# Inverse softmax sums by way of DRAM, K loaded for four heads, q and K turned in pairs

## The chip, the cores and the metric

The kernel runs on one core of one Trainium2 chip. The core has five engines that run side by side: TensorE (PE in the profile, with its weight loads as PEld), VectorE (DVE), ScalarE (ACT), GpSimd (POOL) and SyncE (SP), which issues the DMAs. Sixteen DMA engines carry out what is issued. The metric is the time of the device in microseconds (us), the median of several runs.

## The reference

The kernel computes a banded attention and, on its output, a soft mixture of experts. Cut to what matters:

```
# attention: q, k, v are 4 batches x 8 heads x 768 positions x 64; n_global 8, n_local 96
scores = q @ k.T / 8 + bias            # bias: -slope of the head x distance
scores = where(keep, scores, -1e9)     # keep: key < n_global, or 0 <= row - key < n_local
a = exp(scores - max); a = a / (a.sum(-1) + 1e-9)
x = (a @ v), heads side by side        # 3072 x 512
# experts: 8, each 512 -> 1024 -> 512
P = exp(x @ w_gate - max)
repeat 8 times: P /= rows' sums; P /= columns' sums; P *= N / E
out = sum over e of P[:, e] * (relu(x @ w1[e]) @ w2[e])
```

## The kernel before, in words

**Attention.** Three tiles of 128 query rows of one batch make a unit; there are 8 units (two halves of 768 rows for each of 4 batches). A unit has 4 steps, one for each pair of heads, so there are 32 steps n in all (`self.work`). A step has 3 groups t: group i holds query tile i of both heads. All 96 groups are walked in rounds of two (`CHUNK`), in `Banded.unit` (L357). Query tiles see only the keys near them and the first 32 keys, so a step of the first half needs four key tiles without their last piece, and one of the second half five; `PIECES` lists the row pieces from which the tiles of K and V are put together in SBUF, one DMA for each piece.

Inputs come in float32 with positions on the 128 partitions. q and K have to be turned so that the 64 features of each head lie on the partitions. `prepare` (L253) does this with matmuls against an identity (tile `tp`), copies the result to `qh` or `kh` in a rounded form on ScalarE and puts the rest into `ql` or `kl` on VectorE. One call handles one part: part 0 turns q, part 1 turns K and then loads q and K of step n + 2 (`load_qk`, L220), part 2 does nothing. V comes for four heads at once, for two steps (`load_v`, L237).

A round, in the order in which PE gets it:

1. `ahead`: scores of the two groups that are four groups on (`s_ps`, three matmuls for each product of the rounded parts). `softmax` adds the bias and takes the extreme on VectorE (L313) and the exponential with its row sum on ScalarE (L317). With the last group of a step, ScalarE adds a small number to the six sums of each row (L320), VectorE takes the reciprocal (L321), and ScalarE spreads each of the six values over 64 columns into `inv`, 128 x 384 (L323).
2. `flush`: the product with V of the round before (`o_ps`, L347). With the last group of a step, VectorE multiplies `o_ps` with the inverse sums (L410); ScalarE and VectorE write the result as `xh` and `xl` (L411, L412), the inputs of the experts.
3. `turn` for both groups: the exponentials are turned (`t_ps`), and copied to `pT` on ScalarE or, in the first unit, every second time on VectorE (L340).
4. `between(2)`, then `invert` with the last group of a step: since `o_ps` has the features on the partitions and the positions along the columns, the inverse sums, which have positions on the partitions, are turned too. Three transposes of 128 x 128 into `r_ps` (L419), and a copy back to `inv` on VectorE (L420).
5. `between(1)`, `prepare` of the group that is 8 on; `between(1)`, `prepare` of the one that is 9 on.

The tiles `tp`, `r_ps` and `t_ps` share a tag of two PSUM buffers; in the first unit `tp` and `r_ps` use two buffers of another tag (`self.idle`), which later holds the feed-forward work.

`between` is where other work is put into PE's order: from about the eighth round on, the first experts' products for units that are finished (`h_ps`, `y_ps`: "filler"), a fixed amount for each place, and the gate. It also calls `work()`, which issues up to two spills to DRAM and starts one of the sums and differences of x for the main loop on GpSimd (`combo`, L613 to L617, into the tile `op` with three buffers).

**The order of work.** PE's instructions keep the program's order (`InOrder`). Those of the other engines and the DMA issues, all on SP, are put in order by a scheduler with a simulated time line; each queue then runs strictly in its order, and an instruction that waits holds what stands behind it.

**After attention** the last unit's feed-forward work is done without attention beside it, and then the main loop takes over: for each further pair of column blocks of the experts, a Strassen product of the first layer (`bank_a` to `bank_d`) and the second layer (`y_ps`).

## Time and profile before

| | us |
|---|---|
| median of 3 runs | 2209.69 (2207.13 to 2209.97) |
| profiled execution | 2208.09 |
| its span | 2206.3 |
| busy: PE / PEld | 2181.5 / 1809.1 |
| busy: DVE / ACT / POOL | 1329.7 / 759.4 / 1127.3 |
| first feed-forward matmuls, the gate's | at 60.2 |
| end of attention: its last product with V starts | at 330.0 |
| first bank of the main loop | at 359.4 |

How to read it: an engine's busy time is the time in which it has an instruction under way; matmuls overlap, so a busy PE may still take gaps between starts that a longer or shorter stream would not have. A row of a stretch gives its length, then busy time and number of instructions of each engine, the clock that PE was granted as a share of the full one, the share of time in which the 16 DMA engines were busy, and GB/s. A row of a group gives line, engine, operation, output and inputs, shapes and count; a row of waits gives the waiting engine with its instruction, then what ended the wait, the total in us, how often, and the longest. A row of the time line gives start, duration, engine, line, operation and count. A row of a DMA issue gives its tensors, the number of issues, the size of one and the median time to landing.

### The profile page before, as it was taken

How to read it: one execution, taken by the hardware profiler on the slowest of the kernel's cores; microseconds unless marked ns; L12 is line 12 of the kernel's file. 1: busy time of each engine (PE TensorE's matmuls, PEld its weight loads, DVE VectorE, ACT ScalarE, POOL GpSimd, SP SyncE). 2: the span in 40 equal slices, each digit the busy share in tenths (PEclk: the TensorE clock that was granted, in tenths of full speed). 3: DMA queues.
4: the chain of work that ended last, by engine and by line, in shares of the span. 5: the costliest groups of instructions: out<-in, count | busy, mean ns of one | idle time of the engine just before them, and what ended most of it. 6: DMA issues, size and time to landing. Idle time of an engine off the chain costs nothing.

```text
span 2206.3 us, 29377 instructions
## 1 busy us (share of the span) xinstructions
PE 2181.5 (99%) x10851; PEld 1809.1 (82%) x10851; DVE 1329.7 (60%) x2348; ACT 759.4 (34%) x1540; POOL 1127.3 (51%) x1061
## 2 busy tenths in 40 slices
PE   7999999999999999999999999999999999999999
PEld 5888888888888888888888888888888888888887
DVE  6555545766566666656656666665665666666565
ACT  5667664322222222323222222232242222223221
POOL 5766565445454454545545445455454544545540
PEclk8999999999999999999999999999999999999999
DMA  5665545111111111171111111111611111111111
GB/s 131 176 170 160 143 138 167 48 48 48 58 48 56 50 49 57 48 263 52 48 58 48 56 50 49 57 48 58 199 50 58 48 56 50 49 57 48 58 39 50
DMA packets 207817, 173.47 MB, mean 79 GB/s; under 512 B 102704, under 2 KB 170800, under 8 KB 207664
## 3 DMA queue, kind: packets, MB, share of 16 engines
q1 hardware_dynamic: 207664, 171.51, 25.1%
q8 instruction: 87, 1.43, 0.3%
q14 instruction: 66, 0.54, 0.1%
HBM read 142.36 MB, written 29.10 MB: 78 GB/s over the span
## 4 chain that ended last, share of the span: by engine, by line
PE 96%; ACT 2%; DVE 1%; DMA 1%; issue 0%; POOL 0%; SPq 0%; ACTq 0%; DVEq 0%
PE y_ps L109 46%; PE bank_a L109 11%; PE bank_d L109 11%; PE bank_c L109 11%; PE bank_b L109 5%; PE h_ps L109 2%; PE o_ps L109 2%; PE s_ps L109 2%; PE t_ps L112 2%; PE tp L112 1%; ACT p_sb L317 1%; PE g_ps L109 0%; PE r_ps L112 0%; DVE kl L270 0%; DMA raw_qk<-in_q_dram 0%; PE y_ps L711 0%
## 5 line engine op out<-in xcount | busy, mean ns | idle before, releaser
L996 DVE SCALAR_TENSOR_TENSOR early<-y_ps,pm,early 128x512 f32<-128x512 f32 x672 | 503.0, 749 | 242.3 <-PE y_ps L109 241.6
L569 POOL TENSOR_TENSOR wl<-wsum,wh 128x1280 fp32r<-128x1280 f32 x90 | 266.3, 2959 | 578.0 <-ACT wh L568 578.0
L591 POOL TENSOR_TENSOR wsum<-w1f 128x256 f32<-128x256 f32 x450 | 317.1, 739 | 317.1 <-DMA w1f<-in_moe_w_dram 317.1
L109 PE MATMUL y_ps<-w2h,h_set 128*128 128x512 f32 x1408 | 433.5, 389 | 0.0
L109 PE MATMUL y_ps<-w2h,x 128*128 128x512 f32 x1408 | 433.4, 389 | 0.0
L568 ACT CAST w2h<-w2f 128x1024 fp32r<-128x1024 f32 x90 | 94.8, 1054 | 689.0 <-issue 618.8
L109 PEld LDWEIGHTS y_ps<-w2h,h_set 128*128 128x128 f32 x1408 | 264.3, 188 | 54.9
L109 PEld LDWEIGHTS y_ps<-w2h,x 128*128 128x128 f32 x1408 | 264.3, 188 | 54.9
L109 PE MATMUL y_ps<-w2l,h_set 128*128 128x512 f32 x704 | 274.1, 389 | 0.1
L109 PE MATMUL y_ps<-w2l,x 128*128 128x512 f32 x704 | 273.9, 389 | 0.0
L109 PE MATMUL bank_a<-m,wh 128*128 128x512 f32 x696 | 242.8, 389 | 1.1 <-DVE h_set L641 1.1
L109 PE MATMUL bank_d<-x,wh 128*128 128x512 f32 x696 | 242.7, 389 | 0.0
L109 PE MATMUL bank_c<-x,wh 128*128 128x512 f32 x696 | 242.5, 389 | 0.0
L569 POOL TENSOR_TENSOR w2l<-w2f,w2h 128x1024 fp32r<-128x1024 f32 x90 | 215.9, 2399 | 48.9 <-ACT w2h L568 48.9
L681 DVE TENSOR_TENSOR early<-early,bank_d 128x512 f32<-128x512 f32 x90 | 61.9, 687 | 176.3 <-PE bank_d L109 172.3
L109 PEld LDWEIGHTS y_ps<-w2l,h_set 128*128 128x128 f32 x704 | 132.1, 188 | 27.9 <-DVE early L996 0.5
L109 PEld LDWEIGHTS y_ps<-w2l,x 128*128 128x128 f32 x704 | 132.1, 188 | 27.4
L109 PEld LDWEIGHTS bank_a<-m,wh 128*128 128x128 f32 x696 | 130.6, 188 | 29.0 <-DVE h_set L641 1.9
L109 PEld LDWEIGHTS bank_c<-x,wh 128*128 128x128 f32 x696 | 130.6, 188 | 27.1
L109 PEld LDWEIGHTS bank_d<-x,wh 128*128 128x128 f32 x696 | 130.6, 188 | 27.1
L109 PE MATMUL bank_a<-m,wl 128*128 128x512 f32 x348 | 135.4, 389 | 0.0
L109 PE MATMUL bank_d<-x,wl 128*128 128x512 f32 x348 | 135.4, 389 | 0.0
(233 smaller groups left out, 3494.9 us busy)
## 6 DMA issues: line engine op xcount, KB each, us to landing
w1f<-in_moe_w_dram SPq DMA_DIRECT2D x92, 512.0 KB, 3.5
w2f<-in_moe_w_dram SPq DMA_DIRECT2D x92, 512.0 KB, 3.4
x<-op_m SPq DMA_DIRECT2D x16, 512.0 KB, 7.7
op_m<-op SPq DMA_DIRECT2D x30, 256.0 KB, 2.8
m<-op_m SPq DMA_DIRECT2D x12, 512.0 KB, 7.1
out_dram<-early SPq DMA_DIRECT2D x24, 256.0 KB, 4.0
ys<-y_sb SPq DMA_DIRECT2D x21, 256.0 KB, 3.0
early<-ys SPq DMA_DIRECT2D x21, 256.0 KB, 4.0
```

The source lines that it names most:

```text
L109: return self.tc.keep_in_program_order(self.engine.matmul(*args, **kw))
L112: return self.tc.keep_in_program_order(self.engine.transpose(*args, **kw))
L317: nc.scalar.activation(out=pv, in_=pv, func=AF.Exp, bias=mx[:, u:u + 1], scale=-1.0, accum_out=sm[:, i, j:j + 1])
L568: self.nc.scalar.copy(out=hi, in_=full)
L569: self.nc.gpsimd.tensor_tensor(out=lo, in0=full, in1=hi, op=ALU.subtract)
L591: nc.gpsimd.tensor_tensor(out=s[:, n], in0=x, in1=y, op=op)
L681: tt(out=t3, in0=t3, in1=d, op=ALU.subtract)
L996: nc.vector.scalar_tensor_tensor(out=a, in0=y_ps, scalar=moe.pm[:, tt, e:e + 1], in1=a, op0=ALU.mult, op1=ALU.add)
```

## The change

- The inverse sums are no longer spread over 64 columns, turned on PE and copied back. After the reciprocal, a DMA writes the 128 x 6 values to a DRAM tile of 6 x 128, one value after the other (`turned_sums`); `invert` now issues two DMAs that read three rows of 128 values for one head each and put them on 64 partitions. `inv` is then the tile that L410 multiplies with, as before.
- K is loaded for four heads, that is for two steps, as V was: `load_q` for each step, `load_k` for every second one. Two K buffers and two q buffers take the place of two buffers for both.
- `prepare` turns q and K of a step in one go. The two groups' turns of the exponentials are followed by all the places for other work (2, 1 and 1), and at the end of the round stand the inverse's reads and `prepare`: in three rounds, which make two steps, the first has `invert` of the even step and `prepare` of an odd one, the second `invert` of the odd step, the third `prepare` of an even one.
- The tile `op` of the sums on GpSimd has two buffers in place of three. The data of the warm-up matmuls and the distances of the first tile lie elsewhere in the same memory.

```diff
-    QK, V = UT + 4, 5
-    RAW = QK * P + V * 2 * P
+    Q, K, V = UT * P, 4 * 2 * P, 5 * 2 * P
...
+        self.dram = ctx.enter_context(tc.tile_pool(name="f_inv", bufs=4, space=DRAM))
...
+    def load_q(self, n):
...
+        t = self.early_q if n % 2 == 0 else self.raw.tile([P, self.Q], F32, name="raw_q")
...
+    def load_k(self, n):
...
+        t = self.early_k if n % 4 == 0 else self.raw.tile([P, self.K], F32, name="raw_k")
+        t = t.rearrange("p (t c) -> p t c", c=2 * P)
+        self.load_heads(t, self.k, n, 4, [x for x in PIECES[half] if x[0] != 2 + half], 1)
+        self.ks[n], self.ks[n + 1] = t[:, :, 0:P], t[:, :, P:]
...
-    def prepare(self, t):
-
-
-        n, part = divmod(t, 3)
-        if n >= len(self.work) or part == 2:
+    def prepare(self, n):
+
+        if n >= len(self.work):
             return
...
+        for src, hi, lo, nb in ((q_r, qh, ql, UT), (k_r, kh, kl, UT + self.work[n][1])):
+            tp = self.turned("tp")
+            for t in range(nb):
+                self.pe.transpose(out=tp[:, t], in_=src[:, t], identity=self.ident)
+            tp = tp.rearrange("p t c -> p (t c)")[:, 0:nb * P]
+            nc.scalar.copy(out=hi[:, 0:nb * P], in_=tp)
+            nc.vector.tensor_tensor(out=lo[:, 0:nb * P], in0=tp, in1=hi[:, 0:nb * P], op=ALU.subtract)
+        self.load_q(n + 2)
+        if n % 2:
+            self.load_k(n + 3)
...
             nc.vector.reciprocal(out=sm, in_=sm)
-            self.inv[n] = self.wrk.tile([P, UT, P], F32, name="inv", bufs=3)
-            nc.scalar.copy(out=self.inv[n].rearrange("p t (j d) -> p (t j) d", j=2),
-                           in_=sm.rearrange("p t j -> p (t j)").unsqueeze(2).broadcast_to([P, 2 * UT, D]))
+            self.turned_sums[n] = self.dram.tile([UT * 2, P], F32, name="inv_d")
+            nc.sync.dma_start(out=self.turned_sums[n].rearrange("c p -> p c"), in_=sm.rearrange("p t j -> p (t j)"))
...
         for t in range(u * per, (u + 1) * per, CHUNK):
             self.ahead(range(t + AHEAD, t + AHEAD + CHUNK))
             self.flush()
-            turned = [(t + c, self.turn(t + c)) for c in range(CHUNK)]
-            between(CHUNK)
-            for t1, pT in turned:
+            for t1 in range(t, t + CHUNK):
                 n, group = divmod(t1, NG)
-                if group == NG - 1:
-                    self.invert(n)
                 if group == 0:
                     self.outs[n] = self.ps.tile([P, UT, P], F32, name="o_ps", tag="o", bufs=2)
                 g = n % (self.H // 2)
-                self.pending.append((n, group, pT, self.outs[n], xh[g], xl[g]))
-            for c in range(CHUNK):
-                between(1)
-                self.prepare(t + AHEAD + NG + 1 + c)
+                self.pending.append((n, group, self.turn(t1), self.outs[n], xh[g], xl[g]))
+            for c in (CHUNK, 1, 1):
+                between(c)
+            n = t // NG
+            if t % (2 * NG) == 0:
+                self.invert(n)
+            elif t % (2 * NG) == CHUNK:
+                self.invert(n + 1)
+            if t % (2 * NG) != CHUNK:
+                self.prepare(n + NG)
...
     def invert(self, n):
 
-        inv = self.inv[n]
-        r_ps = self.turned("r_ps")
-        for i in range(UT):
-            self.pe.transpose(out=r_ps[:, i], in_=inv[:, i], identity=self.ident)
-        self.nc.vector.tensor_copy(inv, r_ps[:, 0:UT])
+
+        self.inv[n] = self.wrk.tile([P, UT, P], F32, name="inv", bufs=3)
+        src = self.turned_sums.pop(n).rearrange("(t j) p -> j t p", j=2)
+        for j in range(2):
+            rows = slice(j * self.D, (j + 1) * self.D)
+            self.nc.sync.dma_start(out=self.inv[n][rows], in_=src[j].partition_broadcast(self.D))
...
-        xout = att.enter_context(tc.tile_pool(name="xout", bufs=3))
+        xout = att.enter_context(tc.tile_pool(name="xout", bufs=2))
```

65 lines of the change are left out of this document (25 added, 40 removed).

## The prediction

> **What bounds the kernel now.** I read the split of the time by stretches first, because shares over the whole run mix stages. The stretches are cut at the first matmul of the feed-forward work (62), the end of attention (331) and the start of the main loop (360).
>
> ```profile
> core 0: us, PE busy (x) PEld busy (x) DVE busy (x) ACT busy (x) POOL busy (x), PEclk, DMA share, GB/s
> 0.00:10.00 10.00, 7.01 (x22) 2.63 (x22) 4.87 (x19) 2.35 (x4) 6.75 (x24) 1.00 0.42 90
> 20.00:62.00 42.00, 33.09 (x300) 26.78 (x299) 27.19 (x100) 30.51 (x105) 20.98 (x20) 0.87 0.58 144
> 62.00:331.00 269.00, 266.35 (x2239) 228.15 (x2237) 140.07 (x502) 184.65 (x566) 172.13 (x202) 1.00 0.57 158
> 360.00:2206.00 1846.00, 1839.44 (x8112) 1521.49 (x8111) 1140.66 (x1678) 525.83 (x831) 907.55 (x796) 1.00 0.19 63
> ```
>
> From 62 on TensorE (PE) is never idle for long: 2.65 of 269 us in the attention stage, 6.6 of 1846 us in the main loop. Its order is the program's order, so an instruction taken out of that order shortens the stage by its place in the stream. The stretch 20 to 62 is different: no engine is full (PE 33.1, ScalarE 30.5, VectorE 27.2 of 42 us), and PE's granted clock is 0.87. It is a chain through several engines. The change touches both stretches and nothing after 331.
>
> The waits of PE, first of 0 to 62, then of 62 to 350:
>
> ```profile
> PE s_ps L109 <- DVE kl L270: 6.0, 4, 3.2
> PE tp L112 <- DVE inv L420: 2.8, 2, 2.2
> PE tp L112 <- DMA raw_qk<-in_q_dram: 2.4, 2, 1.3
> PE r_ps L112 <- ACT pT L340: 1.4, 1, 1.4
> PE tp L112 <- DMA raw_qk<-in_k_dram: 0.6, 1, 0.6
> ...
> PE s_ps L109 <- DVE kl L270: 1.8, 7, 0.3
> ```
>
> The last row is all that PE waits for in the stage from 62 to 350. So what can be won there is work of PE itself.
>
> **Removed: the turn of the inverse sums.** The work of r_ps is in 15 instructions before 62 and 81 after it, that is 5 and 27 sets of three. "Busy" counts each matmul until its modelled end, so I take the price from the starts in the stream of PE, around one set:
>
> ```profile
> 0.00:62.00 62.00, 2.51 (x15) 1.74 (x15) 2.75 (x5) 0.86 0.54 130
> 62.00:331.00 269.00, 13.39 (x81) 10.22 (x81) 14.88 (x27) 1.00 0.57 158
> ...
> 201.51 0.33 PE L109 MATMUL h_ps<-x,w1l 128*128 128x384 f32 x1
> 201.69 0.34 PE L109 MATMUL h_ps<-x,w1h 128*128 128x384 f32 x1
> 201.86 0.49 PE L112 MATMUL r_ps<-ident,inv 128*128 128x128 f32 x3
> 202.11 0.42 PE L109 MATMUL h_ps<-x,w1h 128*128 128x384 f32 x1
> 202.37 0.34 PE L109 MATMUL h_ps<-x,w1l 128*128 128x384 f32 x1
> ```
>
> Undisturbed, one h_ps matmul starts 0.175 us after the other (201.51, 201.69). From 201.69 to 202.37 there are two such steps and the set: 0.68 - 2 x 0.175 = 0.33 us. So 27 x 0.33 = 8.9 us leave the stage from 62 to 331. The upper bound is the busy time of that row, 13.4 us. With the set go a copy on ScalarE and one on VectorE, 0.51 and 0.56 us each by the rows below; both engines have slack after 62 (184.7 and 140.1 of 269 us), so they count nothing there and matter only before 62.
>
> ```profile
> L323 ACT COPY inv<-sm x32: 500/512/525, 21.6 to 318.2; 128x384 f32<-128x384 f32 x32
> L420 DVE COPY inv<-r_ps x32: 515/558/558, 28.5 to 328.8; 128x384 f32<-128x384 f32 x32
> ```
>
> **Added: a write of 768 items of 4 bytes and two reads of 192 rows of 512 bytes for each of 32 steps.** No row shows such a write. Three things can cost: the issue on SP, the DMA engines, the way's length.
>
> ```profile
> 152.69 2.38 SPq L218 DMA_DIRECT2D early<-in_k_dram  x5
> ...
> raw_qk<-in_q_dram SPq DMA_DIRECT2D x32, 96.0 KB, 2.9
> n_raw<-in_n_global_dram SPq DMA_DIRECT2D x1, 1.0 KB, 2.6
> ```
>
> *Issue.* One issue takes 2.38 / 5 = 0.48 us of SP. The kernel before issues 5 K loads in a step of the first half and 7 in one of the second: 16 x 5 + 16 x 7 = 192. Loading K for four heads halves that to 96, and 3 x 32 = 96 are added: the sum on SP is zero, if a write of many small items issues like any other. Queued behind a write that waits for its reciprocal, or a read that waits for its write, are loads of q, K and V and spills; a load is issued about two steps ahead (20 us at 269 / 27 = 10 us for a step), so a wait of a microsecond or two at SP's head reaches nobody.
>
> *DMA engines.* In the first 10 us nearly all packets are 256 bytes of q, K and V: 0.42 x 16 x 10 us of engine time over 900 KB / 256 B = 3516 packets gives 19 ns a packet. With 19 ns as the price of a 4-byte item (bounds: 0, and any multiple that latency to DRAM may make of it), a write takes 768 x 19 / 16 = 0.9 us of the 16 engines, and the reads, at up to twice 19 ns a row, 384 x 38 / 16 = 0.9 us. 1.8 us in a step of 10 us lifts the share from 0.57 to 0.75: room is left.
>
> *Length.* The write has 768 items against 384 packets of a q load, which lands after 2.9 us; 1 KB in eight-byte runs takes 2.6 us. I bound the landing by 2.6 and 2 x 2.9 = 5.8 us. In the new order a whole round stands between the last exponentials of a step and the issue of its reads, and another between that and the multiplication L410. A round is two thirds of a step, 10 x 2 / 3 = 6.6 us. Both legs fit, the write at its upper bound by 0.8 us. Were they late, L410 would hold VectorE, behind it the score reductions L313, and by these the exponentials and PE. I take nothing.
>
> **Moved: q and K turned back to back at the end of a round.** Before, K of every second step was turned just ahead of its first scores: that is the wait for kl, 1.8 us after 62. Now a whole round lies between, so it goes. Late next are the two PSUM buffers that the pair fills, which the next round's turns of p_sb want back. The existing cover, by one turn of K and the next turn of p_sb:
>
> ```profile
> 203.42 0.60 PE L112 MATMUL tp<-ident,raw_qk 128*128 128x128 f32 x4
> ...
> 204.05 0.59 ACT L269 CAST kh<-tp 128x512 fp32r<-128x512 f32 x1 [0.64 <-PE tp L112]
> ...
> 204.67 0.69 DVE L270 TENSOR_TENSOR kl<-tp,kh 128x512 fp32r<-128x512 f32 x1 [0.68 <-ACT kh L269]
> ...
> 206.77 1.09 PE L112 MATMUL t_ps<-ident,p_sb 128*128 128x128 f32 x8
> ```
>
> K's buffer is free at 205.36, the next turn starts at 206.77: 1.4 us of slack. A pair adds q's copy ahead of K's on ScalarE, 0.5 us like the copy of inv, which has the same shape, so 0.9 us are left, as long as no other work stands before the two copies on ScalarE, which is busy 69% of this stage. Bounds: 0, and 1 us in each of 27 pairs. I take 1.8 us in all, as much as the kl wait that goes, since the chain has the same two copies and the same slack: net zero, between 1.8 gained and some 25 lost.
>
> **Before 62.** Five sets go: 5 x 0.33 = 1.7 us. The turn of K waited 2.8 us for the inverse's copy on VectorE to give back its buffer; there is no such copy and no third user of these buffers now. The other waits of the list may go as well: q and K loads 3.0 us (SP has 10 issues fewer ahead of the first rounds), pT 1.4, and kl 6.0 - 3.2 = 2.8 (the longest one, 3.2, comes before the first scores and stays). But the exponentials of ScalarE can be what ends each of them next. The clock may give something too:
>
> ```profile
> 51.31 1.97 PE L109 MATMUL o_ps<-pT,raw_v 128*64 128x128 f32 x16
> 53.22 1.70 PE L112 MATMUL t_ps<-ident,p_sb 128*128 128x128 f32 x8
> ...
> 56.44 1.09 PE L109 MATMUL o_ps<-pT,early 128*64 128x128 f32 x16
> 57.47 1.09 PE L112 MATMUL t_ps<-ident,p_sb 128*128 128x128 f32 x8
> ```
>
> After the 2.2 us wait for inv, the same work took (1.97 - 1.09) + (1.70 - 1.09) = 1.5 us more. Bounds of this stretch: 0 (ScalarE holds the chain anyway) and 1.7 + 2.8 + 3.0 + 1.4 + 2.8 + 1.5 = 13.2. I take the two terms whose cause vanishes, and of the other 8.7 us, for which ScalarE stands ready as the next cause, only 0.5: 1.7 + 2.8 + 0.5 = 5.0.
>
> **Other edits.** Two buffers for the combined operands in place of three: the third covers the spill's landing while GpSimd goes on, and GpSimd is busy 172 of 269 us; its one wait of that kind is the row below. Its last sum before the main loop ends at 317.9, 13 us ahead of the end of attention, which is its cover; if PE ends 14 us earlier, these sums are the next thing late, but they are not read by PE before the first bank at 359. I take nothing, with the range's upper side for a backlog. Warm-up data in another place, d0 moved: no instruction more.
>
> ```profile
> POOL op L615 <- DMA op_m<-op: 2.7, 1, 2.7
> 317.16 0.74 POOL L617 TENSOR_TENSOR op<-xsum,op 128x256 fp32r<-128x256 f32 x1
> ```
>
> **Sum.** 8.9 + 0 + 5.0 = 13.9 us. The profiled execution took 2208.1 us (span 2206.3, 1.8 around it): 2194.2. It lies 1.6 us under the median of the runs shown, 2209.7, which makes 2195.8; I forecast **2195**.
>
> **Rivals.**
>
> *The first rounds don't shorten* (18%). For it: the chain there already runs over ScalarE, and a removed wait can return as another. Against it: its inverse copies, 5 x 0.51 us, go from the same chain. Time: 2209.7 - 8.9 = 2201, still faster.
>
> *The pairs eat the gain* (10%), no change. The turns of p_sb wait for the buffers of the q and K pair each time. For it: two buffers, both taken at once, ScalarE 69% busy. Against it: 0.9 us of slack by the rows. At 0.5 us for each of 27 pairs: 2195 + 13.5 = 2208.
>
> *The small items fill the DMA queues* (12%), slower. Place: the write to DRAM, one packet for each 4 bytes. Of 269 - 9 = 260 us of the stage the engines are busy 0.57 x 269 = 153 with what they do now and 27 x 0.9 = 24 with the reads; 83 us are free, 3.1 us for each of 27 writes, which is 3.1 x 16 / 768 = 64 ns an item against the 19 ns of a 256-byte packet. Beyond that point loads fall behind and PE waits for q and K; the gain of 14 us is used up at 64 + 14 x 16 / (27 x 768) ns = 75 ns. At 100 ns the excess is 27 x 768 x 36 / 16 = 47 us: 2195 + 47 = 2242. Against it: the packets of 256 bytes cost so little that size can't be all of their price, and nothing shows a smaller one to cost three times more. The Trainium skill, "DMA: Bandwidth & Descriptors", section "Rules for kernel authors", speaks against the change just here: a strided last dimension makes one descriptor for each element, and a rearranged access pattern is no way to transpose (it gives a factor of 19 against the hardware's transpose). No run here shows that factor; applied to 19 ns it would be far beyond the point.
>
> **How the numbers follow.** Forecast 60%, and the rivals 18, 10 and 12%. A difference of 0.2%, 4.4 us, is about what a measurement of this kernel can tell from no change. The forecast and the first rival are faster by more than that: 78%; the second is the same: 10%; the third slower: 12%. The forecast's own range goes from 2187 (before 62 its upper bound, 8 us more) to 2203; with both first rivals, and a little for the stage's upper bound of 13.4 us, the range is 2185 to 2210, which leaves out the slow case and a tail below.
>
> **What would show it.** PE's stretch up to the end of attention is some 14 us shorter, the stretch from the first bank of the main loop to the end as long as before (2206 - 359 = 1847 us). r_ps and both copies are gone. In the list of waits, L410 doesn't wait for a DMA into inv: the way is hidden. If t_ps waits for ql or kl by more than 5 us in all, the second rival is at work; if tp waits for q or K loads after 62 and the DMA share passes 0.9, the third. The packets below 256 bytes, times the share, give the price of an item. I am wrong if the stage from the first gate to the end of attention isn't shorter by 7 to 13 us.

## The result, and the profile after

The changed kernel is slower. Its median is 2412.7 us (five runs, 2407.0 to 2414.4) against 2209.6 us for the kernel before (five runs): the ratio is 1.092, with a 95% interval of 1.0904 to 1.0934, or 203 us more. The forecast was 2195.

The page of the changed kernel shows where to look. In the chain that ended last, transfers now hold 14% of the span, and the packets below 512 bytes have grown by 24576, which are the 32 x 768 items of the new writes. The packets of the kernel before, then packets and chain of the changed one:

```profile
DMA packets 207817, 173.47 MB, mean 79 GB/s; under 512 B 102704, under 2 KB 170800, under 8 KB 207664
```

```profile
DMA packets 244680, 179.85 MB, mean 75 GB/s; under 512 B 127280, under 2 KB 207664, under 8 KB 244528
PE 81%; DMA 14%; SPq 2%; POOL 1%; DVE 1%; ACT 1%; issue 1%; DVEq 0%; ACTq 0%; POOLq 0%
```

The same stretches as before, cut at 62 and 331 us, with the rest of the longer attention stage up to 560 (columns as in the prediction: length, busy time and instructions of PE, PEld, DVE, ACT and POOL, then PE's granted clock, DMA share, GB/s):

```profile
20.00:62.00 42.00, 20.43 (x196) 16.49 (x195) 16.71 (x69) 17.62 (x67) 11.68 (x12) 0.74 0.62 86
62.00:331.00 269.00, 184.87 (x1321) 157.46 (x1320) 81.81 (x307) 109.81 (x345) 104.11 (x106) 0.80 0.75 112
331.00:560.00 229.00, 161.78 (x1048) 136.51 (x1047) 62.28 (x215) 85.43 (x248) 86.15 (x113) 0.81 0.64 117
```

Before, PE was busy for 266.35 of the 269 us from 62 to 331 and started 2239 matmuls. Now it is busy for 184.87 and starts 1321. No other engine has become full, and the DMA engines move 112 GB/s where they moved 158, although their busy share rises from 0.57 to 0.75. The clock falls to 0.80 as well.

Three groups of matmuls date the loss; a row gives the shortest, median and longest duration in ns, then the first and the last start. First the kernel before: the gate, the main loop's second `bank_a` group (L109), and the last product with V.

```profile
L109 PE MATMUL g_ps<-x,ghl x56: 331/337/422, 60.2 to 304.5; 128*128 128x384 f32 x56
...
L109 PE MATMUL bank_a<-m,wh x696: 389/389/499, 415.3 to 2178.7; 128*128 128x512 f32 x174
...
L109 PE MATMUL o_ps<-pT,raw_v x352: 272/273/473, 39.6 to 330.9; 128*64 128x128 f32 x176
```

Then the changed kernel:

```profile
L109 PE MATMUL g_ps<-x,ghl x56: 331/339/668, 84.6 to 480.9; 128*128 128x384 f32 x56
...
L109 PE MATMUL bank_a<-m,wh x696: 387/389/504, 620.0 to 2383.4; 128*128 128x512 f32 x174
...
L109 PE MATMUL o_ps<-pT,raw_v x352: 272/273/476, 56.5 to 526.5; 128*64 128x128 f32 x176
```

From the first to the last start of `bank_a` both kernels take 1763.4 us, so the main loop is untouched. It begins 204.7 us later. Of that, 24.4 us are lost before the gate, 171.2 from there to the last product with V (195.6 less 24.4), and 9.1 behind it.

The list of waits up to 580 us (waiting instruction, what ended the wait, total us, times, longest):

```profile
DVE o_ps L414 <- DMA inv<-inv_d: 213.7, 21, 21.6
...
POOL op L620 <- DMA op_m<-op: 175.2, 20, 26.5
...
PE t_ps L112 <- DVE ql L274: 53.2, 10, 11.6
```

VectorE's multiplication waits for the inverse by way of DRAM; PE waits for `ql`, which VectorE writes. But GpSimd waits almost as long for spills that have nothing to do with the inverse. The chain of waits around 200 us (start, duration, what) shows how long the legs take:

```profile
193.03 10.80 DMA inv_d<-sm
...
204.48 4.08 DMA inv<-inv_d
...
209.90 11.84 DMA inv_d<-sm
...
222.65 0.38 SPq L328
...
224.73 10.72 DMA inv<-inv_d
```

The two writes of 3 KB take 10.8 and 11.8 us. The read of 10.72 us runs beside the next write, issued by L328 at 222.65. What the engines do meanwhile, in stretches cut by hand ahead of, during and after these writes (columns as above):

```profile
190.00:195.00 5.00, 4.62 (x44) 3.70 (x42) 0.18 (x1) 0.86 (x3) 4.84 (x4) 1.00 0.64 184
196.00:204.00 8.00, 5.62 (x20) 4.20 (x20) 3.14 (x12) 3.89 (x13) 5.13 (x5) 0.79 0.45 29
204.00:212.00 8.00, 2.22 (x13) 1.68 (x15) 1.87 (x4) 2.47 (x6) 3.65 (x5) 0.80 0.85 263
213.00:221.00 8.00, 8.00 (x63) 7.02 (x65) 1.94 (x11) 4.21 (x13) 4.96 (x7) 0.84 0.99 40
224.50:231.00 6.50, 1.18 (x6) 0.85 (x6) 0.00 (x0) 0.00 (x0) 0.00 (x0) 0.86 0.51 34
```

During a write, all sixteen engines together move 29 to 40 GB/s for about 8 us; right after it, 263. The busy share doesn't tell the one from the other (0.45 and 0.99 in two such holds, 0.85 between them); the GB/s do.

### The profile page after: what moved, and what is told of

It reads as the page before. It is cut to its first block, busy times and chain, and to the rows that moved or that the text cites. A ratio compares the mean times of both kernels' runs of the same rounds, so it can differ in the third digit from the quotient of the medians.

```text
span 2411.0 us, 29134 instructions
## 1 busy us (share of the span) xinstructions
PE 2224.7 (92%) x10755; PEld 1843.9 (76%) x10755; DVE 1314.4 (55%) x2316; ACT 747.0 (31%) x1508; POOL 1125.8 (47%) x1061
## 4 chain that ended last, share of the span: by engine, by line
PE 81%; DMA 14%; SPq 2%; POOL 1%; DVE 1%; ACT 1%; issue 1%; DVEq 0%; ACTq 0%; POOLq 0%
PE y_ps L109 40%; PE bank_a L109 10%; PE bank_d L109 10%; PE bank_c L109 10%; PE bank_b L109 5%; DMA inv_d<-sm 4%; DMA inv<-inv_d 3%; DMA op_m<-op 3%; DMA ys<-y_sb 1%; PE h_ps L109 1%; SPq L425 1%; PE s_ps L109 1%; PE t_ps L112 1%; PE o_ps L109 1%; DMA early<-in_v_dram 1%
## 5 line engine op out<-in xcount | busy, mean ns | idle before, releaser
L109 PE MATMUL y_ps<-w2h,h_set 128*128 128x512 f32 x1408 | 433.5, 389 | 0.0
L109 PE MATMUL y_ps<-w2h,x 128*128 128x512 f32 x1408 | 433.5, 389 | 0.0
L109 PEld LDWEIGHTS y_ps<-w2h,x 128*128 128x128 f32 x1408 | 264.3, 188 | 54.8
L109 PEld LDWEIGHTS y_ps<-w2h,h_set 128*128 128x128 f32 x1408 | 264.3, 188 | 54.8
L109 PE MATMUL y_ps<-w2l,h_set 128*128 128x512 f32 x704 | 274.1, 389 | 0.1
L109 PE MATMUL y_ps<-w2l,x 128*128 128x512 f32 x704 | 273.9, 389 | 0.0
L109 PE MATMUL bank_a<-m,wh 128*128 128x512 f32 x696 | 242.8, 389 | 1.0 <-DVE h_set L646 1.0
L109 PE MATMUL bank_d<-x,wh 128*128 128x512 f32 x696 | 242.6, 389 | 0.0
L109 PE MATMUL bank_c<-x,wh 128*128 128x512 f32 x696 | 242.5, 389 | 0.0
L109 PEld LDWEIGHTS y_ps<-w2l,h_set 128*128 128x128 f32 x704 | 132.2, 188 | 27.8 <-DVE early L1001 0.5
L109 PEld LDWEIGHTS y_ps<-w2l,x 128*128 128x128 f32 x704 | 132.2, 188 | 27.4
L109 PEld LDWEIGHTS bank_a<-m,wh 128*128 128x128 f32 x696 | 130.7, 188 | 29.0 <-DVE h_set L646 1.9
L109 PEld LDWEIGHTS bank_c<-x,wh 128*128 128x128 f32 x696 | 130.7, 188 | 27.1
L109 PEld LDWEIGHTS bank_d<-x,wh 128*128 128x128 f32 x696 | 130.6, 188 | 27.0
L414 DVE TENSOR_TENSOR o_ps<-o_ps,inv 128x384 f32<-128x384 f32 x32 | 18.1, 565 | 227.5 <-DMA inv<-inv_d 213.7
L109 PE MATMUL bank_a<-m,wl 128*128 128x512 f32 x348 | 135.4, 389 | 0.0
```

The source lines that it names most:

```text
L109: return self.tc.keep_in_program_order(self.engine.matmul(*args, **kw))
L414: self.nc.vector.tensor_tensor(out=o_ps, in0=o_ps, in1=self.inv.pop(n), op=ALU.mult)
```

## The experiments

Two theories stood at first. **The small items fill the queues** (theory A in the expectations), the prediction's third rival: the write holds up every other transfer, whoever waits for it. **The way is long** (theory B): L410 (L414 here) waits for the inverse and holds VectorE, and the rest follows. A third, theory C, has the pairs or the new order of the loads cost part of it. The diffs are cut to their core; +/- is against the kernel named. Ratios are to the kernel before.

### The change without the way through DRAM

`e1_turn_kept`, against the changed kernel: the inverse is spread and turned on PE as before. K loads, pairs, order and all the rest stay.

```diff
-            self.turned_sums[n] = self.dram.tile([UT * 2, P], F32, name="inv_d")
-            nc.sync.dma_start(out=self.turned_sums[n].rearrange("c p -> p c"), in_=sm.rearrange("p t j -> p (t j)"))
+            self.inv[n] = self.wrk.tile([P, UT, P], F32, name="inv", bufs=3)
+            nc.scalar.copy(out=self.inv[n].rearrange("p t (j d) -> p (t j) d", j=2),
+                           in_=sm.rearrange("p t j -> p (t j)").unsqueeze(2).broadcast_to([P, 2 * UT, D]))
...
+        r_ps = self.turned("r_ps")
+        for i in range(UT):
+            self.pe.transpose(out=r_ps[:, i], in_=inv[:, i], identity=self.ident)
+        self.nc.vector.tensor_copy(inv, r_ps[:, 0:UT])
```

> The changed kernel, but the inverse sums are turned on PE as before (three transposes into r_ps, copy back), so there is no way through DRAM; K for four heads, turns in pairs, two buffers for op stay. Theory A (the small writes hold up the DMA engines) and theory B (only the length of the way holds VectorE) both expect the loss to go: the 8.9 us of the removed turns are not won, the first rounds win 0 to 8 us: 2200 to 2211. Theory C (the pairs or the new order of loads cost part of the 203 us) expects 2230 or more.

Measured: 2195.3 us, ratio 0.9942 (0.9925 to 0.9958). It beats both kernels, and lies 5 us below what any of the three theories expected; theory C is out. Its windows:

```profile
20.00:62.00 42.00, 35.95 (x363) 29.69 (x360) 31.06 (x116) 35.22 (x120) 26.71 (x28) 0.99 0.76 185
62.00:331.00 269.00, 269.00 (x2241) 233.18 (x2240) 138.71 (x496) 185.07 (x562) 175.19 (x201) 1.00 0.57 163
```

PE has no idle time from 62 to 331, and the chain before 62 runs faster. So the whole loss, 217 us, hangs on the way through DRAM, and the rest of the change gains 13 us.

`e2_way_alone`: the kernel before with the write, the two reads and nothing else of the change.

```diff
-            nc.scalar.copy(out=self.inv[n].rearrange("p t (j d) -> p (t j) d", j=2),
-                           in_=sm.rearrange("p t j -> p (t j)").unsqueeze(2).broadcast_to([P, 2 * UT, D]))
+            nc.sync.dma_start(out=self.turned_sums[n].rearrange("c p -> p c"), in_=sm.rearrange("p t j -> p (t j)"))
...
-            self.pe.transpose(out=r_ps[:, i], in_=inv[:, i], identity=self.ident)
-        self.nc.vector.tensor_copy(inv, r_ps[:, 0:UT])
+            self.nc.sync.dma_start(out=self.inv[n][rows], in_=src[j].partition_broadcast(self.D))
```

> The kernel before, with nothing changed but the inverse sums' way: one write of 768 items of 4 bytes and two reads for each step. Theories A and B expect nearly the whole loss here, 2370 to 2450, and theory B rather more than the changed kernel has, because the reads are issued in the same round as the step's last turns and have less than a round. Theory C expects clearly less than the changed kernel's 2412.

Measured: 2447.9 us, ratio 1.1084 (1.1062 to 1.1106). In the old order the way costs 240 us over the kernel before (2208.0 in the runs beside it), more than the 217 of the new order.

### The other parts

`e10_pairs_alone` (the kernel before with q and K turned in pairs and the new order of a round) and `e11_k_for_four_alone` (K for four heads, two `op` buffers, the moved data).

```diff
e10, against the kernel before:
-            turned = [(t + c, self.turn(t + c)) for c in range(CHUNK)]
...
-                self.prepare(t + AHEAD + NG + 1 + c)
+            between(CHUNK)
+            if t % (2 * NG) == 0:
+                self.invert(n)
+            elif t % (2 * NG) == CHUNK:
+                self.invert(n + 1)
+            for c in (1, 1):
+                between(c)
+            if t % (2 * NG) != CHUNK:
+                self.prepare(n + NG)
e11, against the kernel before:
-            self.load_qk(n + 2)
+            self.load_q(n + 2)
+            if n % 2:
+                self.load_k(n + 3)
...
-        xout = att.enter_context(tc.tile_pool(name="xout", bufs=3))
+        xout = att.enter_context(tc.tile_pool(name="xout", bufs=2))
```

> The kernel before with nothing changed but the order: q and K of a step turned together at the ends of rounds, turns of the exponentials ahead of all the other work; inverse turned on PE, K loaded for two heads, three buffers for op. If the order is what gains e1's 12.7 us (the scores no longer wait for kl: 75 ns from one start of s_ps to the next before, 62 in e1, 418 times, 5.4 us; and in the first rounds less waits), 2195 to 2199. If K for four heads is needed for the first rounds (10 issues fewer on SP ahead of them), 2200 to 2204.

> The kernel before with nothing changed but the loads (K for four heads, q by itself) and two buffers for op, which its memory needs. If the order is what gains, 2205 to 2210; if the loads gain in the first rounds, 2200 to 2204.

Measured: the pairs 2200.5 us, ratio 0.9963 (0.9949 to 0.9977); the loads 2208.6, ratio 1.0001 (0.9991 to 1.0010). The order alone gives 8 us, the loads alone nothing, both together 13. The difference lies ahead of the gate, which starts at 58.0 us with the pairs alone, at 60.7 with the loads alone and at 54.1 in e1. Part of where the 8 us come from shows in the first of the three matmuls of a score product (median duration, 378 ns in the kernel before, then the same row with the pairs alone):

```profile
L109 PE MATMUL s_ps<-kl,qh x152: 275/378/386, 62.8 to 313.4; 64*128 64x256 f32 x128, 64*128 64x128 f32 x24
```

```profile
L109 PE MATMUL s_ps<-kl,qh x148: 219/326/384, 66.8 to 304.6; 64*128 64x256 f32 x124, 64*128 64x128 f32 x24
```

52 ns less, 148 times, is 7.7 us of durations, but matmuls overlap: the busy time of all score matmuls from 62 to 331 falls from 39.69 us for 456 of them to 35.51 us for 444, which is 3.1 us for as many. With the 2.65 us in which PE had been idle, that is 5.8 us. The windows with the pairs alone, from the gate to the last product with V and from there to the second `bank_a` group:

```profile
58.00:322.00 264.00, 264.00 (x2242) 229.04 (x2242) 138.05 (x501) 183.00 (x566) 179.84 (x208) 1.00 0.59 162
322.00:406.40 84.40, 84.12 (x390) 70.41 (x387) 51.53 (x117) 31.08 (x52) 47.60 (x44) 1.00 0.38 123
```

The first stretch took 330.9 - 60.2 = 270.7 us in the kernel before, 6.7 more; the second took 84.4 as well; and the gate starts 2.2 us earlier. That shorter score matmuls and the idle time make most of the 6.7 us is worked out from these rows and not tested by itself.

### Who is hurt by the write

`e3_write_unread`: e1, with the same write of 768 items in each step, which nothing reads.

```diff
+            copy_d = self.dram.tile([UT * 2, P], F32, name="inv_d")
+            nc.sync.dma_start(out=copy_d.rearrange("c p -> p c"), in_=sm.rearrange("p t j -> p (t j)"))
```

> As e1 (inverse sums turned on PE and used from there), and beside it the same write of 768 items of 4 bytes to DRAM for each step, which nobody reads or waits for. Theory A: after each of the 32 writes the DMA engines move some 35 GB/s in place of some 150 for 8 us, about 6.4 us lost each, 205 us in all; the stage before needed 0.57 of 331 us, 189 us, so 394 us are needed and the stage can't end before that: 2270 or more, and PE, VectorE or ScalarE wait for loads and spills. Theory B: nobody waits for the inverse, so the time is that of e1, 2200 to 2215.

Measured: 2347.4 us (two runs, 2341.9 and 2353.0), ratio 1.0629 (1.0599 to 1.0659). A write that nobody reads costs 152 us over e1. Its window and one of its waits:

```profile
62.00:331.00 269.00, 213.79 (x1584) 182.57 (x1585) 101.31 (x365) 134.66 (x410) 119.16 (x126) 0.86 0.74 116
```

```profile
PE tp L112 <- DMA raw_q<-in_q_dram: 56.1, 10, 13.2
```

PE now waits for q itself: other transfers are held up. Theory A takes 152 of the 217 us. There is a second way in which the write delays them, on SP:

```profile
SPq L223 <- DMA inv_d<-sm: 67.0, 19, 7.7
```

L223 issues loads of K and V, which read nothing of this write. Each of the 19 waits stands at the eighth DMA that SP issues after the write: in this program a late write also stops the queue eight issues later. How the 152 us divide between this and slower transfers, no run tells apart.

`e13_inverse_of_step_before` tests theory B from the other side. It is the changed kernel, but the multiplication takes the inverse of the step before, which has had a whole step more to arrive (and `inv` has four buffers in place of three).

```diff
-        self.nc.vector.tensor_tensor(out=o_ps, in0=o_ps, in1=self.inv.pop(n), op=ALU.mult)
+        self.nc.vector.tensor_tensor(out=o_ps, in0=o_ps, in1=self.inv[n] if n < 1 else self.inv.pop(n - 1), op=ALU.mult)
```

> The changed kernel with its write of 768 items and both reads for each step, but the multiplication of o_ps takes the inverse of the step before (the first step its own), so that the way has a step more to arrive; the outputs are scaled by the wrong sums. It needs four buffers of inv in place of three. If the 65 us between e3 (2347) and the changed kernel (2412) are the wait for a late inverse, that wait goes and the held-up queues stay: e3's time less the turns, 8.9 us, plus the reads' load: 2330 to 2365. If the reads' own load on the queues makes the 65 us, 2390 or more.

Measured: 2406.4 us, ratio 1.0892 (1.0861 to 1.0924). The wait of VectorE falls by two thirds and the time stays:

```profile
DVE o_ps L414 <- DMA inv<-inv_d: 73.8, 7, 22.5
...
PE tp L112 <- DMA raw_q<-in_q_dram: 65.9, 11, 9.9
```

So the 213.7 us at L414 were the wait that happened to come last; with most of it gone, PE's wait for q has grown from 11.5 us in the changed kernel to 65.9.

### What in the write is dear

All of the next six are e3 with the unread write going elsewhere; each has 768 items of 4 bytes, read from the same place.

```diff
-            copy_d = self.dram.tile([UT * 2, P], F32, name="inv_d")
-            nc.sync.dma_start(out=copy_d.rearrange("c p -> p c"), in_=sm.rearrange("p t j -> p (t j)"))
e6, to SBUF, 8 bytes apart:
+            copy_s = self.wrk.tile([P, UT * 2, 2], F32, name="inv_s", bufs=4)
+            nc.sync.dma_start(out=copy_s[:, :, 0], in_=sm.rearrange("p t j -> p (t j)"))
e7, to DRAM in the order of SBUF, 8 bytes apart:
+            copy_d = self.dram.tile([P, UT * 2, 2], F32, name="inv_d")
+            nc.sync.dma_start(out=copy_d[:, :, 0], in_=sm.rearrange("p t j -> p (t j)"))
e14, to DRAM, turned, 8 bytes apart (e15: 4 for the 2, 16 bytes; e12: 16, 64 bytes; e8: P, 512 bytes):
+            copy_d = self.dram.tile([UT * 2, P, 2], F32, name="inv_d")
+            nc.sync.dma_start(out=copy_d[:, :, 0].rearrange("c p -> p c"), in_=sm.rearrange("p t j -> p (t j)"))
```

> As e3 (inverse sums turned on PE, an unread copy beside), but the 768 items of 4 bytes are written to SBUF, 8 bytes apart, and not to DRAM. Theory A1 (DRAM as target makes a small write dear): the time of e1, 2193 to 2205, and no stretch of 8 us with 35 GB/s behind a write. Theory A2 (any item of 4 bytes is dear for the DMA engines): as e3, 2320 to 2370.

> As e3, but the 768 items go to DRAM in the order in which they lie in SBUF, 8 bytes apart: each partition has a block of 48 bytes of its own, so that items of 16 partitions no longer share 64 bytes. Theory A1a (writes from several DMA engines to the same few bytes of DRAM wait for each other) expects 2195 to 2250, between e1 and e3. Theory A1b (each small write to DRAM has its price, wherever it lands) expects e3's time, 2320 to 2370.

> As e3, but each of the 768 items has 512 bytes of DRAM for itself. Theory A1a expects e1's time, 2193 to 2215. Theory A1b expects e3's, 2320 to 2370, or more.

> As e3 and e8 (an unread write of 768 items of 4 bytes to DRAM), but each item has 64 bytes of DRAM for itself. If writes wait for each other only within some 64 bytes: e8's time, 2193 to 2200. If the block in which they wait is of 512 bytes, as 8 items would share it: like e7, 2215 to 2240.

> As e3 (unread write of 768 items, values of neighbouring partitions side by side), but each item 8 bytes from the next, so that 64 bytes hold 8 items, of 8 partitions, in place of 16. If the number of items in a block of 64 bytes sets how long the queues are held (16: 8 us, 8 in e7: 3 to 4 us, 1: nothing), the time is near e7's: 2215 to 2250, with a hold of 4 us. If it matters that e7's items of one block come from one or two partitions, it stays near e3: 2290 or more.

> As e14 with 16 bytes from item to item, 4 items in 64 bytes. By the number of items in a block, a hold of 2 us, which the loads can bear: 2195 to 2215.

Measured, one run each (e3 two), against e1's 2195.3, whose four runs spread over 1.1 us; landing is the median time from a write's issue to its landing, which e3's trace doesn't give (e18 below has the same write):

| where the items go | items in 64 bytes of DRAM | landing, us | us | over e1 |
|---|---|---|---|---|
| adjacent in DRAM (e3) | 16 | 11.4 (e18) | 2347.4 | 152 |
| DRAM, 8 bytes apart, SBUF's order (e7) | 8 | 6.0 | 2226.1 | 31 |
| DRAM, 8 bytes apart, turned (e14) | 8 | 5.7 | 2203.5 | 8 |
| DRAM, 16 bytes apart (e15) | 4 | 3.9 | 2196.2 | 1 |
| DRAM, 64 bytes apart (e12) | 1 | 3.4 | 2195.4 | 0 |
| DRAM, 512 bytes apart (e8) | 1 | 3.1 | 2195.8 | 0 |
| SBUF, 8 bytes apart (e6) | none | 2.5 | 2195.4 | 0 |

The 64 bytes are a yardstick: what the runs vary is the distance, and no run shows the size of a block within which writes disturb each other. With the distance grows the range over which a write is spread, too, from 3 KB in e3 to 384 KB in e8. A narrow range alone isn't what costs: e4 below writes the same 3 KB in 128 pieces, and it lands after 3.1 us. Whether many writes to one block or many writes to one narrow range are to blame isn't separated.

The kernels e3 and e12 are the cleanest pair: the same instructions, packets, sizes and bytes. Queue row of e3, then of e12 (packets, MB, share of the 16 engines' span):

```profile
q1 hardware_dynamic: 231216, 171.60, 29.8%
```

```profile
q1 hardware_dynamic: 231216, 171.60, 25.9%
```

Only the addresses differ, and 152 us with them. The records of single packets in these two traces show where the time goes. The write's own 4-byte packets take 9 ns at the median in e3 and 7 in e12, and nine tenths of a write's items start within about 0.5 us in both. But of some 80,000 packets of 256 bytes (from 20 us to 12 us after the last write), 1402 take longer than 300 ns in e3, the longest 5.5 us; in e12 it is 4, the longest 0.4 us. So the items don't fill the engines by their own time: packets of other transfers stall. The changed kernel has the same: 9 ns for an item, 1366 such packets, the longest 5.2 us.

The stretches after one write each, in e3, e14, e15 and e12 in this order (3 us beginning 2.5 us after the issue and, where there are two rows, the next 4 us):

```profile
194.80:197.80 3.00, 3.00 (x39) 2.53 (x38) 2.29 (x9) 1.75 (x5) 0.00 (x0) 1.00 1.31 47
197.80:201.80 4.00, 3.93 (x26) 3.58 (x23) 2.14 (x7) 3.52 (x12) 0.00 (x0) 1.00 1.37 29
```

```profile
204.97:207.97 3.00, 3.00 (x17) 2.49 (x17) 0.66 (x2) 2.86 (x10) 2.92 (x3) 1.00 0.29 67
207.97:211.97 4.00, 4.00 (x44) 3.35 (x42) 3.03 (x11) 2.90 (x11) 3.84 (x4) 1.00 1.04 297
```

```profile
204.16:207.16 3.00, 3.00 (x17) 2.46 (x16) 1.49 (x3) 2.98 (x10) 0.47 (x1) 1.00 0.59 129
```

```profile
204.25:207.25 3.00, 3.00 (x17) 2.47 (x16) 1.48 (x3) 2.98 (x10) 0.47 (x1) 1.00 0.69 152
```

With 16 items in 64 bytes the traffic stays at 29 to 47 GB/s through both stretches; with 8 it is at 67 in the first and back at 297 in the second; with 4 it is at 129, not far below the 152 with one, which is about what the stage moves anyhow. In the rows of e14, e15 and e12 PE has no idle time; in e3's it has next to none yet, and stands later, when loads come late.

e14 lost less than expected; the other five lie where their first theory had put them (A1 for e6, A1a for e7 and e8). e7 and e14 have the same number of items in 64 bytes and differ by 23 us; why the order of the items makes that difference wasn't settled.

### Two other ways to DRAM, and a way without it

`e4_runs_of_24_bytes`: the changed kernel with the six values of a partition side by side in DRAM, 128 runs of 24 bytes in place of 768 of 4; the reads are the same, so they fetch the values in another order.

```diff
-            nc.sync.dma_start(out=self.turned_sums[n].rearrange("c p -> p c"), in_=sm.rearrange("p t j -> p (t j)"))
+            nc.sync.dma_start(out=self.turned_sums[n].rearrange("c p -> (c p)").rearrange("(p c) -> p c", p=P),
+                              in_=sm.rearrange("p t j -> p (t j)"))
```

> The changed kernel, but each partition writes its six values in one run of 24 bytes: 128 items in place of 768 for the same 3 KB; the reads are as in the changed kernel, so they fetch the values in another order, and the outputs are scaled by the wrong sums. By theory A with a price for each item (8.5 us x 16 / 768 = 177 ns), a write takes 128 x 177 / 16 = 1.4 us of the engines, and the time is near what was forecast for the change: 2190 to 2215. If the bytes or the touched lines of DRAM set the price, the loss stays: over 2350. Theory B: the write lands in some 3 us, the way fits: 2190 to 2215 too.

`e5_one_turn_rows_to_dram`: one transpose on PE, 128 x 6 to 6 x 128, and six rows of 512 bytes to DRAM; the reads as in the change.

```diff
+        r_ps = self.turned("r_ps").rearrange("p t c -> p (t c)")[0:2 * UT, 0:P]
+        self.pe.transpose(out=r_ps, in_=self.sums[n].rearrange("p t j -> p (t j)"), identity=self.ident)
+        flat = self.wrk.tile([2 * UT, P], F32, name="flat", bufs=2)
+        self.nc.vector.tensor_copy(flat, r_ps)
+        self.nc.sync.dma_start(out=self.turned_sums[n], in_=flat)
```

> The changed kernel, but the 128 x 6 inverse sums are first turned by one PE transpose to 6 x 128, copied to SBUF, and written to DRAM as 6 rows of 512 bytes; the reads are as in the changed kernel. If it is the 768 small items that cost (theory A), nothing is left of the loss: one turn in place of three takes some 0.11 us in place of 0.33, so 32 x 0.22 = 7 us below e1's 2195, and a copy less on ScalarE: 2184 to 2192. If a way through DRAM by itself holds VectorE (theory B; the 24-byte runs left 43 us of such waits), it is above 2200, and L414's multiplication waits for the reads of inv.

`e9_scaled_before_turn`: e1 without any inverse to turn; VectorE multiplies the exponentials with their reciprocals while positions are still on the partitions.

```diff
+        for u, pv in enumerate(views):
+            nc.vector.tensor_scalar(out=pv, in0=pv, scalar1=sm[:, i, u:u + 1], scalar2=None, op0=ALU.mult)
...
-        self.nc.vector.tensor_tensor(out=o_ps, in0=o_ps, in1=self.inv.pop(n), op=ALU.mult)
```

> As e1, but there is no inverse to turn at all: after each group's exponentials VectorE takes the reciprocals of its two sums for each row and multiplies the exponentials by them, where the sums still lie on the partitions of the rows; r_ps, inv, both its copies and the multiplication of o_ps are gone. PE loses all 32 sets of r_ps, 10.6 us; VectorE gets some 0.9 us for each group in place of 1.3 for each step, 1.4 us more in a step of 10 us, and has room after 62 us (139 of 269 us busy in e1). Before the first gate VectorE is busier (31 of 42 us in e1), which may cost some 3 to 6 us there. 2183 to 2192. If VectorE's order holds up the scores, it is 2195 or more.

Measured: e4 2211.4 us, ratio 1.0013 (1.0004 to 1.0023); e5 2206.6, 0.9992 (0.9983 to 1.0001); e9 2231.2, 1.0106 (1.0089 to 1.0123). e4 lies where both theories put it. e5 and e9 missed their main expectations on the slow side and lie where the second ones put them: e5 above 2200, with L418 (L414 of the changed kernel) waiting 14.6 us for the inverse, as theory B has it, and e9 above 2195.

In e4 the hold is gone and with it 201 us, but the way is still no gain: it is 16 us behind e1, and the multiplication waits still, though its writes land after 3.1 us at the median (its waits; then issue to landing of the write):

```profile
DVE o_ps L414 <- DMA inv<-inv_d: 43.1, 14, 7.6
```

```profile
DMA to landing us min/median/max: 1.8/3.1/5.9
```

e5 loses at both ends. Its gate starts at 63.4, against 54.1 in e1; the chain before 62 runs over the way (chain of waits of e5):

```profile
26.32 4.05 DMA inv_d<-flat
...
31.12 2.94 DMA inv<-inv_d
...
49.05 2.09 DMA inv_d<-flat
...
51.79 4.36 DMA inv<-inv_d
```

13.4 us of these stand in the way there, where nothing else is full. The stage after the gate then gives an estimate of what the removed transposes are worth. From the gate to the last product with V, and from there to the second `bank_a` group, first e1, then e5:

```profile
54.10:318.10 264.00, 264.00 (x2241) 229.03 (x2241) 138.06 (x501) 182.91 (x566) 174.40 (x202) 1.00 0.55 156
318.10:402.50 84.40, 84.12 (x390) 70.38 (x387) 51.59 (x117) 31.09 (x52) 47.87 (x44) 1.00 0.38 123
```

```profile
63.40:323.50 260.10, 259.48 (x2190) 221.16 (x2190) 131.42 (x501) 172.54 (x542) 172.80 (x202) 1.00 0.64 179
323.50:412.60 89.10, 86.12 (x391) 71.32 (x388) 51.61 (x117) 30.87 (x52) 47.66 (x44) 0.98 0.38 123
```

51 matmuls fewer shorten the attention stage by 3.9 us, 76 ns each, or 89 ns if PE's 0.6 us of idle time is taken off. The stretch behind it is 4.7 us longer, with PE idle for 3.0 of its 89.1 us.

In e9, VectorE is busy for 40.53 of the 42 us before the gate and for 224.98 of 269 after it, and PE is busy for 242.73. Before the gate VectorE is the bound; that its order holds up PE after it, too, fits these rows and isn't shown by them.

```profile
20.00:62.00 42.00, 34.48 (x286) 28.40 (x285) 40.53 (x147) 26.32 (x87) 21.80 (x20) 0.79 0.71 170
62.00:331.00 269.00, 242.73 (x1971) 207.02 (x1969) 224.98 (x696) 159.42 (x490) 165.55 (x190) 0.96 0.51 142
```

### The rest of the loss

e3 leaves 65 us of the 217 open. Either SP, which waits for a late write ahead of the reads, holds the queue, or the reads themselves cost.

`e16_reads_of_step_before`: the changed kernel; the reads fetch what the step before had written, to free SP from waiting.

```diff
-        src = self.turned_sums.pop(n).rearrange("(t j) p -> j t p", j=2)
+        src = (self.turned_sums[n] if n < 1 else self.turned_sums.pop(n - 1)).rearrange("(t j) p -> j t p", j=2)
```

> The changed kernel with its 32 writes and 64 reads, but the two reads of a step fetch what the step before wrote (the first step its own), so that SP doesn't stand at them until the write just issued has landed (140 us in 19 waits in the changed kernel, 138 us in e13); the outputs are scaled by the wrong sums. If SP standing there, with the loads behind it, makes the 65 us above e3's 2347: 2330 to 2365. If the reads' own transfers do: 2390 or more, as in e13.

Measured: 2412.7 us, ratio 1.0923 (1.0891 to 1.0954). SP's waits at the reads' line, first the changed kernel, then e16:

```profile
SPq L425 <- DMA inv_d<-sm: 140.2, 19, 9.9
```

```profile
SPq L425 <- DMA inv_d<-sm: 109.1, 15, 10.3
```

The edit didn't take the wait away. In 14 of the 15 waits, the reads stand for the very write that they fetch: with the older write to read, SP's order has them ahead of the next write, mostly three to five issues behind their own. The run tells nothing about SP.

`e17_unread_reads`: e1 with two loads more in each step, of the reads' shape, from q, which nobody uses. `e18_unread_write_and_reads`: e3 with the same two loads. In neither does a load depend on a write or anyone wait for the inverse.

```diff
+        got = self.wrk.tile([P, UT, P], F32, name="got", bufs=1)
+        for j in range(2):
+            rows = slice(j * self.D, (j + 1) * self.D)
+            src = self.q[b, 2 * g + j].rearrange("(x w) d -> x (w d)", w=2)[0:2 * UT:2]
+            self.nc.sync.dma_start(out=got[rows], in_=src.partition_broadcast(self.D))
```

> As e1 (inverse turned on PE), and beside it two loads for each step of the size and shape of the reads (three rows of 512 bytes to 64 partitions each), here of rows of q, that nobody uses; no small write. If the reads' transfers alone make the 65 us: 2230 or more. If they cost only where the queues are held up: e1's time, 2193 to 2202.

> As e17 and e3 together: the unread write of 768 items of 4 bytes and the two unused loads for each step; no load depends on a write, and nobody waits for the inverse from DRAM. If the 65 us come from 64 more DMAs in a stage that the held queues already limit, 2390 to 2430. If they need the dependency (reads that wait for the write, or a multiplication that waits for the reads), e3's time: 2340 to 2360.

Measured: e17 2243.1 us, ratio 1.0153 (1.0124 to 1.0183), 48 us over e1. e18 2419.0 us, ratio 1.0950 (1.0918 to 1.0982), 72 us over e3. Window and SP's wait of e17:

```profile
62.00:331.00 269.00, 234.17 (x1893) 201.84 (x1893) 119.67 (x437) 159.04 (x492) 153.26 (x177) 0.92 0.57 158
```

```profile
SPq L431 <- DMA got<-in_q_dram: 45.4, 26, 3.5
```

Unread transfers alone, 32 writes and 64 loads, lose as much as the changed kernel: 2419.0 against 2412.7. But e17 and e18 have a wait of their own. With one buffer for `got` each load waited for the one before, and SP stood 45.4 us at that line in e17, about as much as e17 lost, and 45.2 us in e18. The transfers as such are not what e17 paid for: no packet of 256 bytes took over 84 ns there from 62 to 330, and e4, which has two such reads a step with three buffers, and a write, is only 16 us over e1. So e18 shows that the wait at L414 and the wait of a read for its write aren't needed for a loss of this size; it doesn't show that they had no part in the changed kernel's. Whether the last 65 us there are SP's standing (140.2 us at the reads, and 47.4 us at L223 as in e3), the late inverse or the reads' transfers beside the hold, no run tells apart.

## Why the prediction was wrong, by its steps

- **What bounds the kernel** held: PE's own stream in the attention stage. e1 and e10, with PE busy for all 269 us, gained in this stage what their stream became shorter. But "what can be won there is work of PE itself" left out that an edit can add waits from engines that had slack, above all the DMA engines.
- **Added, DMA engines: failed, and this step decides.** It priced the write by the engine time of its items, 19 ns each, the price of a 256-byte packet of a load, and put nothing for what the items do to other transfers. Their own time was less than that, 9 ns. But behind each write other packets stalled, and the traffic was down to 29 to 40 GB/s for about 8 us. Spread over the items, such a hold is 8 x 16 / 768 = 167 ns of an engine for each; e3's loss gives a like size by the rival's own sum, (152 / 32 + 3.1) x 16 / 768 = 164 ns. The price isn't one of size or number: the same items 64 bytes apart, or to SBUF, cost nothing. It goes with their distance in DRAM. The busy share of 0.75 that this step forecast came to the hundredth, by luck: it meant more traffic than the 158 GB/s of before, and there were 112. The last 65 us, after e3's 152, came with the reads; how stays open.
- **Added, length: failed.** The landing was bounded by 2.6 and 5.8 us, from the loads. The legs of the chain were 10.8 and 11.8 us for the write, 4.1 and 10.7 for the reads. Even without the hold (e4, landing at 3.1 us) the multiplication waited 43.1 us in all: "both legs fit" was wrong by more than the write. By e13 this lateness isn't what sets the time of the changed kernel.
- **Added, issue: not as predicted.** "The sum on SP is zero" held for the count, but "a wait of a microsecond or two at SP's head reaches nobody" met waits of up to 9.9 us, 140.2 us in all. In e3, loads that have nothing to do with the write stood 67.0 us behind it.
- **Removed: not reached, and probably priced too high.** 0.33 us a set is 110 ns a transpose; e5 gives 76 to 89 ns for each of 51. For 81 that is 6 to 7 us in place of 8.9, an estimate from e5's stage after the gate. No kernel here has the sets gone and the gain kept.
- **Moved: put at nothing, and it gained.** I let 1.8 us gained and 1.8 lost cancel. The pairs gained 6.7 us after the gate and nothing was lost: PE's idle time went, and the first score matmul, which had been 52 ns longer than it need be, became shorter (worked out, not tested); only the 1.8 us of the wait for `kl` had been counted. The second rival, that the pairs eat the gain, is out: its sign came in the changed kernel, where `t_ps` waits 53.2 us for `ql`, but e1 has the same pairs and no idle time of PE.
- **Before 62: right in size in e1, 6.1 us (60.2 to 54.1) where 5.0 was forecast, but not for the reasons given,** since the sets and both copies are still there. So the size was luck. The pairs alone give 2.2 (58.0); the other 3.9 come with K's loads beside them. In the changed kernel, these rounds lost 24.4 us: their chain ran over the way, as e5's did. The first rival, that they do not shorten, had the wrong reason too.
- **Other edits: right.** e11 is within 0.1% of the kernel before.
- **Rival 3 had the place and the consequence**, the write to DRAM with loads falling behind, and its test of PE waiting for q came true in e3 (in the changed kernel that wait was 11.5 us). It was given 12%. Its mechanism was another, engines filled by the time of the items, and at the 100 ns for an item that it took it reached 2242. Its sign for the DMA share, above 0.9, did not come: the share rose to 0.75 only.

The Trainium skill, "DMA: Bandwidth & Descriptors", section "Rules for kernel authors", which the prediction set against its own sum, was right about this change: one descriptor for each element, to be avoided. The reason isn't the number of descriptors alone, though: e12 has as many as e3 and costs nothing. The Trainium skill, "DMA: Bandwidth & Descriptors", section "Specifications", says that transfers below 512 bytes are done by reading, changing and writing back. Items close together in DRAM having to wait for each other would fit that, and e3, e14, e15 and e12 agree in that a greater distance costs less; but items 64 bytes apart are as small, and cost nothing here. That the engines do so is not shown by these runs.

## What to carry to other kernels

Don't scatter many 4-byte items next to each other in DRAM: 768 of them held up the core's other transfers for some 8 us, and whoever needed a load waited, not only the reader of the items. The same items 16 bytes or more apart, or the same 3 KB in runs of 24 bytes, held up next to nothing here. Where a turn by way of DRAM is priced, take the price from a run with the write alone, unread, and look at the GB/s after it, not at the busy share. And count the duration of a matmul against its like, not only the engine's idle time, when judging what a better order can give.

## What the runs showed that I had not expected

- The cost of a write of 768 items of 4 bytes goes with their distance in DRAM: 152 us for 32 writes with the items side by side, 8 and 31 at 8 bytes, 1 at 16, 0 at 64 and at 512, 0 to SBUF.
- During such a hold the busy share of the DMA engines is anything (0.45 to 1.37 in the rows above), so it shows neither that they are free nor that they are full. The items' own packets are no slower in it than elsewhere; the others' are.
- A write to DRAM that nothing reads, in a stage where PE never waited for a transfer, cost 152 us. Two loads of 96 KB more in each step, with one buffer that each had to wait for, cost 48.
- Taking away the longest wait of the list, two thirds of 213.7 us, changed the time by 6 us: the wait that is named is the last one, not the one that sets the pace.
